# Dynamic convolution into a gated MLP on one core: tiles taken from 8 on, group 0 one step ahead of group 1, all seven taps added by TensorE

## Chip, core and metric

The kernel runs on one NeuronCore of a Trainium2 chip. The metric is the device time of one execution, in microseconds; lower is better. The time before the change is 1306.71 us, the median of 3 runs (1306.46 to 1307.04).

## What is computed

The input `x` is 4 batches of 4096 positions of 192 numbers. For each position and each of 8 heads, seven weights are made by a softmax, and the 24 numbers of the head are the weighted sum of the last seven positions. The result goes, as 16384 tokens of 192 numbers, through a gated MLP with 1536 hidden units. The weights of the MLP arrive as float64.

```python
w = exp(weight_gen - max(weight_gen, axis=-1))          # [4, 4096, 8, 7]
w = w / (sum(w, axis=-1) + 1e-9)
x_pad = concatenate([zeros(B, 6, D), x], axis=1)
att[b, s, h, :] = sum over k of w[b, s, h, k] * x_pad[b, s + k, h, :]
g, v = att @ w_gate, att @ w_val                        # 192 -> 1536
out = (g * sigmoid(g) * v) @ w_out                      # 1536 -> 192
```

## The kernel before

**Tiles.** Partition p holds the 128 consecutive tokens 128p to 128p+127; tile t is token t of every partition, so there are 128 tiles of 128 tokens, and a tap's earlier position is the tile before, in the same partition. Tiles 0 to 5 need the last six tiles of the partition before (the halo, PAD = 6); at the start of a batch the halo is zero. Four tiles (JG) make a group; there are 32 groups. `x` is loaded in chunks of 8 tiles (`load_x`), the softmax weights in chunks `wcuts` of 12 and then 24 tiles (`load_taps`).

**Steps.** The hidden units are cut into 12 blocks (NF) of 128. One step (g, f) takes block f of group g: `up_first` and `up_second` make 18 matmuls in row pairs into two PSUM banks (of four, so two steps are in flight), ScalarE does `silu` (L522), VectorE multiplies (`gated`, L531 for groups 0 and 1, L536 after them), and two steps later (LAG) `down` (L570 for groups 0 and 1, L581 and L590 after them) adds the block into the output. The list `steps` gives the order: with HEAD = 4, group 0 takes four steps alone, then groups 1 and 0 take turns, and from step 24 on groups 2 to 31 follow one by one.

**What lies beside the steps.** `todo[i]` is a list of small operations that are issued with step i: the first through `between` ahead of the step's product on VectorE, the others after it. Every engine works in the order of issue. The lists hold: the conversion of a weight block from float64 (`weight_ops`: five parts, six instructions on VectorE and three on ScalarE, L415 to L474, and the load of the block four further on); `split` of the output weights (L405, L406); the attention of the next group on VectorE (`attention_ops`: seven products at L230 and six additions at L251) with its transposition through DRAM (`turn_ops`); the softmax of the next chunk (`softmax_ops`); and loads. The exponentials of a chunk stand together in one step (`exps`), since they need another table on ScalarE than silu.

**Groups 0 and 1** are transposed by TensorE instead (`summed_turn`): VectorE makes a tap's product into a tile `xatt` (three buffers), ScalarE copies 64 of its columns to the end (`twice`, L304), and `turn` (L309) multiplies its four tiles by the identity in 8 matmuls (16 records in the trace) that add into two PSUM banks. `SUMS` says which taps VectorE adds first: group 0 has five turns for seven taps (two additions, L300), group 1 has four (three additions). `split_ops` then makes the high part (ScalarE, L370) and the low part (VectorE, L377) of the sum.

**The prologue** is everything issued before step 0: the loads, the softmax of the first chunk, the taps of group 0 with weight block 0 between them, and block 1 and part of 2. In before, group 1's taps lie in steps 0 to 3. The first chunk of `x` needs its halo at once: four memsets on GpSimd (L149) and eight DMAs (L152).

Of the kernel before, what the change touches and what calls it, by code (L numbers as in the profile page):

```python
# [18 lines left out]
def dynconv_glu_kernel(  # L19
# [41 lines left out]
    EXP1 = 16  # L61
    LOAD1 = 1
# [3 lines left out]
    HEAD = 4  # L66
    SUMS = {0: ((0,), (1,), (2,), (3, 4), (5, 6)), 1: ((0, 1), (2, 3), (4, 5), (6,))}
# [39 lines left out]

    xcuts = cut([2 * JG])
    wcuts = cut([3 * JG, 6 * JG])
# [10 lines left out]
    def load_taps(c):  # L120

        j0, n = wcuts[c]
        wt = w_t[c] = soft.tile([P, NJ, H, K], F32, tag="wt", name="wt")
        pieces = {0: (0, JG, n), 1: range(0, n + 1, 2 * JG)}.get(c, (0, n))

        def load(a, b):
            nc.sync.dma_start(
                out=wt[:, a:b].rearrange("p t h k -> p t (h k)"), in_=wgr[:, j0 + a : j0 + b]
            )

        return [lambda a=a, b=b: load(a, b) for a, b in zip(pieces, pieces[1:])]

    def load_x(c):

        j0, n = xcuts[c]
        xt = x_t[c] = xin.tile([P, PAD + NX, D], F32, tag="xt", name="xt")
        pieces = {0: (0, JG, n), 1: range(0, n + 1, 2)}.get(c, (0, n))

        def load(a, b):
            own = PAD if c and a == 0 else 0  # L140
            nc.sync.dma_start(
                out=xt[:, PAD + a - own : PAD + b], in_=xr[:, j0 + a - own : j0 + b]
            )
            if c == 0 and a == 0:
# [3 lines left out]
                for p0 in range(0, P, per):  # L148
                    nc.gpsimd.memset(xt[p0 : p0 + 1, 0:PAD], 0.0)  # L149
# [8 lines left out]
    def softmax_ops(c):  # L158
# [3 lines left out]
        def cuts(m):  # L162
            return [slice(j, min(j + m, n)) for j in range(0, n, m)]
# [44 lines left out]
        if c == 0:  # L208
            before = [
                op  # L210
                for p in (slice(0, JG), slice(JG, n))
                for op in each(p, (largest, less, exponentials))
            ]
        else:
            before = [op for p in cuts(PIECE) for op in each(p, (largest, less))]
        after = [op for p in cuts(PIECE if c else JG) for op in each(p, (total, inverse, normal))]
# [57 lines left out]
    def summed_turn(g):  # L274
# [6 lines left out]

        parts = SUMS[g]

        def tap(n):
            a = {}

            def product(k, first):
                def go():
                    if first:
                        a["sum"] = att.tile([P, JG, 2 * P], F32, tag="xatt", name="xatt", bufs=3)  # L290
                        mul(nc.vector, k, a["sum"][:, :, 0:D])
                    else:
                        a["other"] = att.tile([P, JG, D], F32, tag="prod", name="prod")
                        mul(nc.vector, k, a["other"])

                return go

            def add():
                x = a["sum"][:, :, 0:D]
                nc.vector.tensor_tensor(out=x, in0=x, in1=a.pop("other"), op=ALU.add)  # L300

            def twice():
                x = a["sum"]
# [252 lines left out]
    def down(g, f, pair, second):  # L556
# [49 lines left out]
        if lo is None:  # L606
            if pair:
# [5 lines left out]
                nc.sync.dma_start(out=outr[:, g * JG : (g + 1) * JG], in_=osb[:, :, 0:D])  # L613
# [14 lines left out]
        for t in range(JG):  # L628
            nc.sync.dma_start(
                out=blocks[:, t0:t1, g * JG + t], in_=osb[t * Q : (t + 1) * Q, t0:t1, 0:D]  # L630
# [12 lines left out]
    with tc.manual_schedule():  # L643
        nc.gpsimd.memset(exp_bias, -920.0 * TWO23)

        load_weights(0, nc.scalar)
        nc.scalar.activation(out=warm, in_=exp_bias, func=AF.Exp)
        now, soon = load_x(0)
        for op in load_taps(0) + [now]:
            op()  # L650
        load_weights(1)
        soon()
# [5 lines left out]
        for op in before:  # L658
            op()
        convert = [weight_ops(f) for f in range(NF)]  # L660
        w0, w1, w2, w3 = convert[:4]
        nc.scalar.activation(out=warm, in_=exp_bias, func=AF.Silu)
        for op in after[:6]:
            op()
        ps, taps = summed_turn(0)

        def tap(n):
            made, turn = taps[n]
            return made + [turn]

        turns = split_ops(0, ps)
# [122 lines left out]
```

## Time and profile before

| | us |
|---|---|
| median of 3 runs | 1306.71 |
| the profiled execution | 1305.82 |
| its span, first to last instruction | 1304.0 |
| TensorE busy | 1271.4 |
| VectorE busy | 1015.6 |
| ScalarE busy | 577.6 |

The profile is of one execution. PE is TensorE's matmuls, PEld its weight loads, DVE is VectorE, ACT ScalarE, POOL GpSimd, SP the queue that issues most DMAs. A matmul's end is modelled, and two matmuls of a row pair run beside each other, so a busy TensorE is not by itself a TensorE at its peak; the distance from one step's first matmul to the next step's is the sounder measure. The granted clock of TensorE has two levels, 1.00 (2.4 GHz) and 0.50 (1.2 GHz).

### The profile page before, as it was taken

To read this page: it belongs to the slowest core of one execution; us is meant where nothing else is said; L and a number is where in the kernel's file an instruction comes from. 1 tells how busy PE (TensorE), PEld (TensorE's weight loads), DVE (VectorE), ACT (ScalarE), POOL (GpSimd) and SP (SyncE) were. 2 spreads that over 40 slices of the span, in tenths; PEclk is the share of its full clock that TensorE was granted. 3 is DMA by queue.
4 is the path that set the end of the run, shared out by engine and by line. 5 is a ranking of instruction groups with operands and counts; after the bars stand their busy time and mean duration, and the time that the engine had idled before them with its cause. 6 is when DMAs were issued, how large, how long until landed. Compare 5 with 4: busy or idle time off the path is not lost.

```text
span 1304.0 us, 31222 instructions
## 1 busy us (share of the span) xinstructions
PE 1271.4 (97%) x13200; PEld 1226.0 (94%) x13200; DVE 1015.6 (78%) x1438; ACT 577.6 (44%) x1010; POOL 4.9 (0%) x11
## 2 busy tenths in 40 slices
PE   4998999999999999999999999999999999999997
PEld 3787988999999999999999999999999999999997
DVE  7798688777788877788877778877778877777843
ACT  3344344544444445444444544444454444444443
POOL 1000000000000000000000000000000000000000
PEclk9899999999999999999999999999999999999999
DMA  5332211212212121211212121121211212111010
GB/s 161 115 102 63 84 29 27 84 29 84 63 33 65 42 71 42 84 47 31 82 30 83 42 73 37 48 78 36 84 42 26 71 42 72 42 42 42 17 38 13
DMA packets 64149, 74.88 MB, mean 57 GB/s; under 512 B 6924, under 2 KB 53516, under 8 KB 62216
## 3 DMA queue, kind: packets, MB, share of 16 engines
q1 hardware_dynamic: 63416, 72.30, 20.1%
q8 instruction: 103, 1.69, 0.5%
q10 hardware_dynamic: 592, 0.59, 0.2%
q14 instruction: 38, 0.31, 0.1%
HBM read 48.48 MB, written 24.38 MB: 56 GB/s over the span
## 4 chain that ended last, share of the span: by engine, by line
PE 86%; DVE 8%; ACT 3%; DMA 2%; issue 1%; SPq 0%; ACTq 0%; DVEq 0%
PE up L502 22%; PE up L514 22%; PE dn L581 20%; PE up L505 18%; PE dn L590 3%; DVE prod L230 1%; DVE h L536 1%; PE dn L570 1%; DVE xatt L230 1%; DVE hi L531 1%; ACT sg L522 1%; DVE e L450 1%; DVE m L439 1%; DVE w L461 1%; ACT L522 0%
## 5 line engine op out<-in xcount | busy, mean ns | idle before, releaser
L581 PE MATMUL dn<-wo,hi 64*128 64x384 f32 x2880 | 550.6, 344 | 0.4 <-ACT hi L537 0.4
L590 PE MATMUL dn<-wo,lo 64*128 64x192 f32 x2880 | 485.4, 249 | 0.3 <-DVE lo L539 0.3
L581 PEld LDWEIGHTS dn<-wo,hi 64*128 64x128 f32 x2880 | 445.8, 184 | 8.8 <-ACT osb L619 1.4
L590 PEld LDWEIGHTS dn<-wo,lo 64*128 64x128 f32 x2880 | 427.4, 186 | 3.2 <-DVE lo L539 0.5
L536 DVE TENSOR_TENSOR h<-up,sg 128x512 f32<-128x512 f32 x360 | 247.6, 688 | 179.3 <-ACT sg L522 179.1
L537 ACT ACTIVATE hi<-h 128x512 fp32r<-128x512 f32 x360 | 227.7, 633 | 358.7 <-DVE h L536 358.6
L522 ACT ACTIVATE sg<-up 128x512 f32<-128x512 f32 x384 | 228.3, 594 | 305.5 <-PE up L514 296.8
L539 DVE TENSOR_TENSOR lo<-h,hi 128x512 fp32r<-128x512 f32 x360 | 246.3, 684 | 80.2 <-ACT hi L537 80.2
L502 PE MATMUL up<-xhi,w_hi 64*128 64x512 f32 x768 | 214.9, 420 | 7.1 <-ACT sg L522 2.5
L514 PE MATMUL up<-xhi,w_hi 64*128 64x512 f32 x768 | 213.3, 421 | 0.2
L505 PE MATMUL up<-xhi,w_hi 64*128 64x512 f32 x768 | 202.0, 391 | 2.0 <-ACT xhi L370 2.0
L502 PE MATMUL up<-xhi,w_lo 64*128 64x512 f32 x768 | 203.7, 395 | 0.0
L502 PE MATMUL up<-xlo,w_hi 64*128 64x512 f32 x768 | 202.6, 391 | 0.3 <-DVE xlo L377 0.2
L505 PE MATMUL up<-xhi,w_lo 64*128 64x512 f32 x768 | 201.9, 391 | 0.0
L514 PE MATMUL up<-xhi,w_lo 64*128 64x512 f32 x768 | 201.3, 390 | 0.0
L505 PE MATMUL up<-xlo,w_hi 64*128 64x512 f32 x768 | 201.1, 388 | 0.2 <-DVE xlo L377 0.2
L514 PE MATMUL up<-xlo,w_hi 64*128 64x512 f32 x768 | 200.5, 387 | 0.0
L230 DVE TENSOR_TENSOR prod<-xt,wt 128x768 f32<-128x768 f32 x185 | 175.7, 950 | 0.2
L251 DVE TENSOR_TENSOR xatt<-xatt,prod 128x768 f32<-128x768 f32 x180 | 170.7, 948 | 0.0
L502 PEld LDWEIGHTS up<-xhi,w_hi 64*128 64x128 f32 x768 | 120.7, 184 | 11.3 <-ACT w_hi L470 3.5
L505 PEld LDWEIGHTS up<-xhi,w_hi 64*128 64x128 f32 x768 | 120.7, 185 | 6.8 <-ACT xhi L370 2.5
L505 PEld LDWEIGHTS up<-xlo,w_hi 64*128 64x128 f32 x768 | 120.9, 185 | 4.7 <-DVE xlo L377 0.5
(54 smaller groups left out, 1246.9 us busy)
## 6 DMA issues: line engine op xcount, KB each, us to landing
xt<-in_x_dram SPq DMA_DIRECT2D x14, 1344.0 KB, 7.2
turned<-cut SPq DMA_DIRECT2D x120, 96.0 KB, 2.0
out_dram<-osb SPq DMA_DIRECT2D x116, 96.0 KB, 1.9
t<-turned SPq DMA_DIRECT2D x60, 128.0 KB, 2.7
t<-turned SPq DMA_DIRECT2D x30, 256.0 KB, 3.0
raw<-in_moe_w_out_dram SPq DMA_DIRECT2D x11, 192.0 KB, 2.7
wt<-in_weight_gen_dram SPq DMA_DIRECT2D x3, 672.0 KB, 4.6
raw<-in_moe_w_gate_dram SPq DMA_DIRECT2D x11, 128.0 KB, 2.2
```

What stands on the lines that cost most here:

```text
L230: engine.tensor_tensor(out=into.rearrange("p t (h i) -> p t h i", h=H), in0=src, in1=w, op=ALU.mult)
L251: nc.vector.tensor_tensor(out=a, in0=a, in1=tmp.pop(k), op=ALU.add)
L439: nc.vector.scalar_tensor_tensor(out=st["m"], in0=st["raw"][:, :, 0], scalar=28, in1=st["m"], op0=ALU.logical_shift_right, op1=ALU.bitwise_or,
L502: nc.tensor.matmul(ps, w[r, fs], m[r], start=(n == 0), stop=False)
L505: ins = nc.tensor.matmul(sums[i], w[r, i, fs], m[r], start=False, stop=False)
L514: ins = nc.tensor.matmul(sums[i], w[r, i, fs], m[r], start=False, stop=(n == len(full) - 1))
L522: nc.scalar.activation(out=sg, in_=sums[0], func=AF.Silu)
L536: nc.vector.tensor_tensor(out=h, in0=sums[1], in1=sg, op=ALU.mult)
L537: nc.scalar.activation(out=hi, in_=h, func=AF.Copy)
L539: nc.vector.tensor_tensor(out=lo, in0=h, in1=hi.bitcast(F32), op=ALU.subtract)
L581: nc.tensor.matmul(acc[g, t], hi[r, cs], wo[r, f].rearrange("p a d -> p (a d)"), start=opens, stop=False,)
L590: nc.tensor.matmul(acc[g, t][:, 0:D], lo[r, cs], wo[r, f, 0], start=False, stop=closes)
```

## The change

- **Order of the tiles.** `place` adds 8 tiles (TURN), modulo 128. Group 0 takes tiles 8 to 11, and its halo is tiles 2 to 7 of the same partition, loaded with them. Tiles 0 to 7, with the halo from the partition before, are the last chunk; its zeros are a memset on VectorE.
- **Order of the steps.** HEAD is 1: (0,0), (1,0), (0,1), (1,1) and so on. A weight block then serves two steps in a row from the start. In step 0 the first six operations of its list go ahead of the product (FIRST).
- **Taps of groups 0 and 1.** No additions on VectorE: seven products, seven copies and seven turns for each group. Group 1's first three products are issued ahead of step 0, everything else of its taps, its `split_ops` and weight block 1 in step 0.
- **Softmax.** The first chunk has 24 tiles, the next two 28, the last two 24. All exponentials of the first chunk are in the prologue, in slices of 4, 4, 8 and 8 tiles, and the silu table is loaded after them. The normalisation of the last two slices lies in steps 1 to 7. The next chunk's softmax lies in steps 31 to 56, its load at step 12.
- **Output weights.** `split` of block f moves to step 23 + f.
- **Start.** ScalarE's first table load comes ahead of its five weight DMAs; SP's order is two pieces of softmax weights, two of `x`, weight block 1, the rest of `x` and of the softmax weights, blocks 2 and 3.

```diff
-    EXP1 = 16
-    LOAD1 = 1
+    TURN = 2 * JG
-    HEAD = 4
-    SUMS = {0: ((0,), (1,), (2,), (3, 4), (5, 6)), 1: ((0, 1), (2, 3), (4, 5), (6,))}
+    HEAD = 1
+    FIRST = 6
+    def place(at):
+        return (at + TURN) % T
-    wcuts = cut([3 * JG, 6 * JG])
+    wcuts = cut([6 * JG, 7 * JG, 7 * JG, 6 * JG])
...
-        pieces = {0: (0, JG, n), 1: range(0, n + 1, 2)}.get(c, (0, n))
+        pieces = {0: (0, JG + 1, PAD + JG, PAD + n), 1: range(0, PAD + n + 1, 2)}.get(c, (0, PAD + n))
+        if at == 0:
+            pieces = (PAD, PAD + n)
...
-            if c == 0 and a == 0:
+            if at == 0:
-                for p0 in range(0, P, per):
-                    nc.gpsimd.memset(xt[p0 : p0 + 1, 0:PAD], 0.0)
+                nc.vector.memset(xt[:, 0:PAD], 0.0)
...
-            made = [product(k, m == 0) for m, k in enumerate(parts[n])]
-            return made + [add] * (len(made) - 1) + [twice], turn
+            return [product, turn]
-        return ps, [tap(n) for n in range(len(parts))]
+        return ps, [tap(n) for n in range(K)]
...
-            while between() and g == 0 and f < HEAD:
-                pass
+            for _ in range(FIRST if g == 0 and f < HEAD else 1):
+                between()
...
+        nc.scalar.activation(out=warm, in_=exp_bias, func=AF.Exp)
         load_weights(0, nc.scalar)
-        nc.scalar.activation(out=warm, in_=exp_bias, func=AF.Exp)
-        now, soon = load_x(0)
-        for op in load_taps(0) + [now]:
+        taps_in, x_in = load_taps(0), load_x(0)
+        for op in (*taps_in[0:2], *x_in[0:2]):
             op()
         load_weights(1)
-        soon()
+        for op in (x_in[2], taps_in[2]):
+            op()
...
+        for op in before[0:6] + after[0:3]:
             op()
         for op in (
-            tap(0) + w0[0:1] + tap(1) + w0[1:2] + tap(2) + w0[2:4] + tap(3) + w0[4:5]
-            + tap(4) + w1[0:3] + turns[0:2] + w1[3:4] + turns[2:4] + w1[4:5] + w2[0:2]
+            taps[0] + w0[0:1] + taps[1] + after[3:6] + taps[2] + w0[1:2] + taps[3] + taps[4] + w0[2:3]
+            + taps[5] + taps[6] + w0[3:4] + before[6:7] + split_ops(0, ps) + w0[4:5] + before[7:]
         ):
             op()
+        nc.scalar.activation(out=warm, in_=exp_bias, func=AF.Silu)
...
+        for tap in taps1[:3]:
+            tap[0]()
+        todo[0] = [tap[1] for tap in taps1[:3]] + [op for tap in taps1[3:6] for op in tap]
+        todo[0] += w1[0:1] + taps1[6]
+        todo[0] += w1[1:3] + split_ops(1, ps1) + w1[3:5]
...
+        spread(load_x(1), 0, 4)
+        todo.setdefault(1, []).extend(after[6:9])
+        spread(after[9:], 3, 9)
         for f in range(NF):
-            todo.setdefault(max(due[f] + 3, HEAD + 6), []).append(
+            todo.setdefault(2 * NF - 1 + f, []).append(
                 lambda f=f: split(wo[:, f, 0], wo[:, f, 1], wo32[:, f])
             )
+        todo.setdefault(NF, []).extend(load_taps(1))
         for c in range(1, len(wcuts)):
-            s0 = (wcuts[c - 1][0] // JG - 1) * NF - LEAD if c > 1 else NF
+            s0 = max((wcuts[c - 1][0] // JG - 1) * NF - LEAD, 2 * NF + 4)
...
-            if i in turns:
-                turns[i]()
```

## Rows read from the trace of the kernel before

**Rows 1.** The page, part 1: busy time, share of the span and instructions.
```profile
PE 1271.4 (97%) x13200; PEld 1226.0 (94%) x13200; DVE 1015.6 (78%) x1438; ACT 577.6 (44%) x1010; POOL 4.9 (0%) x11
```

**Rows 2.** Engines by stretch: length, busy time and instructions, granted clock, DMA.
```profile
30.00:40.00 10.00, 8.29 (x36) 6.34 (x38) 9.68 (x14) 3.03 (x7) 0.00 (x0) 0.54 0.22 62
...
100.00:110.00 10.00, 6.32 (x55) 4.81 (x54) 6.58 (x13) 6.78 (x9) 0.00 (x0) 1.00 0.00 2
...
160.00:180.00 20.00, 20.00 (x212) 17.92 (x211) 19.01 (x27) 9.76 (x19) 0.00 (x0) 1.00 0.12 47
...
260.00:280.00 20.00, 19.77 (x206) 18.80 (x204) 12.53 (x18) 10.20 (x16) 0.00 (x0) 1.00 0.23 52
```

**Rows 3.** Timeline: start, length, instruction; first matmuls of steps 0, 4, 12, 18, 20, 24.
```profile
24.66 0.50 PE L502 MATMUL up<-xhi,w_hi 64*128 64x512 f32 x2
...
54.52 0.51 PE L502 MATMUL up<-xhi,w_hi 64*128 64x512 f32 x2 [1.11 <-ACT xhi L370]
...
81.98 0.53 PE L502 MATMUL up<-xhi,w_hi 64*128 64x512 f32 x2
...
108.42 0.50 PE L502 MATMUL up<-xhi,w_hi 64*128 64x512 f32 x1 [2.53 <-ACT sg L522]
...
116.45 0.54 PE L502 MATMUL up<-xhi,w_hi 64*128 64x512 f32 x2
...
129.93 0.53 PE L502 MATMUL up<-xhi,w_hi 64*128 64x512 f32 x2
```

**Rows 4.** Timeline of the prologue, up to the split of group 0's sum.
```profile
3.59 4.96 SPq L152 DMA_DIRECT2D xt<-in_x_dram  x8
...
7.21 0.39 DVE L200 TENSOR_TENSOR wt<-wt,sm 128x224 f32<-128x224 f32 x1
...
10.60 0.96 DVE L230 TENSOR_TENSOR xatt<-xt,wt 128x768 f32<-128x768 f32 x1 [1.48 <-DMA raw<-in_moe_w_gate_dram]
...
12.12 6.91 PEld L309 LDWEIGHTS tr<-ident,xatt 128*128 128x128 f32 x48 [12.12 <-issue]
...
22.67 2.05 PE L309 MATMUL tr<-ident,xatt 128*128 128x128 f32 x16 [1.15 <-ACT xatt L304]
...
23.87 0.60 ACT L370 ACTIVATE xhi<-tr 128x512 fp32r<-128x512 f32 x1 [0.58 <-PE tr L309]
```

**Rows 5.** Weight loads of turns: mean (13 to 14 us), two timelines, clock by stretch.
```profile
L309 PEld LDWEIGHTS tr<-ident,xatt 128*128 128x128 f32 x7 | 1.6, 333 | 0.0
...
33.15 3.49 PEld L309 LDWEIGHTS tr<-ident,xatt 128*128 128x128 f32 x16 [2.32 <-ACT xatt L304]
...
45.82 1.86 PEld L309 LDWEIGHTS tr<-ident,xatt 128*128 128x128 f32 x16 [0.22 <-issue]
...
39.00:39.25 0.25, 0.25 (x4) 0.07 (x2) 0.25 (x1) 0.00 (x0) 0.00 (x0) 0.72 0.00 0
```

**Rows 6.** Groups by shape, 0 to 115 us: busy us, mean ns, idle before.
```profile
L531 DVE TENSOR_TENSOR hi<-up,sg 128x512 f32<-128x512 f32 x19 | 13.0, 685 | 6.5 <-ACT sg L522 6.3
...
L230 DVE TENSOR_TENSOR xatt<-xt,wt 128x768 f32<-128x768 f32 x10 | 9.5, 952 | 1.5 <-DMA raw<-in_moe_w_gate_dram 1.5
...
L439 DVE SCALAR_TENSOR_TENSOR m<-raw,m 128x576 int32<-128x576 int32 x12 | 9.0, 750 | 0.1
...
L474 DVE TENSOR_TENSOR w_lo<-w,w_hi 128x384 fp32r<-128x384 f32 x12 | 6.7, 555 | 2.4 <-ACT w_hi L470 2.4
L415 DVE TENSOR_SCALAR e<-raw 128x576 int32<-128x576 int32 x12 | 5.4, 453 | 0.0
...
L377 DVE TENSOR_TENSOR xlo<-tr,xhi 128x512 fp32r<-128x512 f32 x4 | 2.7, 688 | 3.5 <-ACT xhi L370 3.5
...
L177 DVE TENSOR_TENSOR wt<-wt,mx 128x448 f32<-128x448 f32 x1 | 0.6, 624 | 0.0
```

**Rows 7.** ScalarE's timeline around the exponentials of step 16: the two table loads.
```profile
103.84 1.28 ACT L183 ACT_TABLE_LOAD   x1
...
106.48 1.28 ACT L522 ACT_TABLE_LOAD   x1
```

More of the change, by code (lines that the diff above doesn't have):

```diff
@@ L123, in load_taps @@
         wt = w_t[c] = soft.tile([P, NJ, H, K], F32, tag="wt", name="wt")
-        pieces = {0: (0, JG, n), 1: range(0, n + 1, 2 * JG)}.get(c, (0, n))
+        pieces = {0: (0, JG, 2 * JG, n), 1: (0, n // 2, n)}.get(c, (0, n))
+        wrap = T - TURN - j0
+        if 0 < wrap < n:
+            pieces = (0, wrap, n)
         def load(a, b):
+            at = place(j0 + a)
             nc.sync.dma_start(
-                out=wt[:, a:b].rearrange("p t h k -> p t (h k)"), in_=wgr[:, j0 + a : j0 + b]
+                out=wt[:, a:b].rearrange("p t h k -> p t (h k)"), in_=wgr[:, at : at + b - a]
             )
@@ L160, in softmax_ops, with cuts @@
         n = wcuts[c][1]
-        def cuts(m):
-            return [slice(j, min(j + m, n)) for j in range(0, n, m)]
+        def cuts(m, first=0):
+            edges = [j for j in (0, first) if j < m] if first else [0]
+            edges = sorted({*edges, *range(0, n, m), n})
+            return [slice(j, k) for j, k in zip(edges, edges[1:])]
         st = {}
@@ L210, in softmax_ops @@
                 op
-                for p in (slice(0, JG), slice(JG, n))
+                for p in cuts(2 * JG, JG)
                 for op in each(p, (largest, less, exponentials))
@@ L215, in softmax_ops @@
             before = [op for p in cuts(PIECE) for op in each(p, (largest, less))]
-        after = [op for p in cuts(PIECE if c else JG) for op in each(p, (total, inverse, normal))]
+        after = [op for p in (cuts(PIECE) if c else cuts(2 * JG, JG)) for op in each(p, (total, inverse, normal))]
         return before, exponentials, after
@@ L280, in summed_turn, with product @@
             ps = [ps_dn.tile([P, NC], F32, tag=f"dn{2 + n}", name=f"tr{n}") for n in range(2)]
-        parts = SUMS[g]
         def tap(n):
             a = {}
[L287 to L303, printed above, removed]
+            def product():
+                a["tap"] = att.tile([P, JG, 2 * P], F32, tag="xatt", name="tap", bufs=3)
+                x = a["tap"]
+                mul(nc.vector, n, x[:, :, 0:D])
                 nc.scalar.activation(out=x[:, :, D:], in_=x[:, :, P:D], func=AF.Copy)
             def turn():
+                x = a["tap"]
                 for half in (1, 0):
@@ L629, in down @@
             nc.sync.dma_start(
-                out=blocks[:, t0:t1, g * JG + t], in_=osb[t * Q : (t + 1) * Q, t0:t1, 0:D]
+                out=blocks[:, t0:t1, place(g * JG) + t], in_=osb[t * Q : (t + 1) * Q, t0:t1, 0:D]
             )
@@ L657, in dynconv_glu_kernel @@
         before, exponentials, after = softmax_ops(0)
-        for op in before:
-            op()
[L660 to L671, printed above, removed]
+        convert = [weight_ops(f) for f in range(NF)]
+        w0, w1 = convert[:2]
+        ps, taps = summed_turn(0)
+        for op in before[0:6] + after[0:3]:
+            op()
         for op in (
-            tap(0) + w0[0:1] + tap(1) + w0[1:2] + tap(2) + w0[2:4] + tap(3) + w0[4:5]
-            + tap(4) + w1[0:3] + turns[0:2] + w1[3:4] + turns[2:4] + w1[4:5] + w2[0:2]
+            taps[0] + w0[0:1] + taps[1] + after[3:6] + taps[2] + w0[1:2] + taps[3] + taps[4] + w0[2:3]
+            + taps[5] + taps[6] + w0[3:4] + before[6:7] + split_ops(0, ps) + w0[4:5] + before[7:]
         ):
             op()
+        nc.scalar.activation(out=warm, in_=exp_bias, func=AF.Silu)
         steps = [(0, f) for f in range(HEAD)]
```

30 lines of the change are left out of this document (10 added, 20 removed).

## The prediction

> **What bounds the kernel now.** I read the page's busy shares first, then the engines by stretch, then TensorE's timeline for the start of each step, and last the timelines of the other engines in the first 110 us. TensorE is busy 97% of the span [rows 1], so a gain can only come from stretches in which it isn't at its pace. By stretches, everything from step 24 on is full: 160 to 180 us shows 20.00 of 20 us while VectorE does 19.01 beside it [rows 2]. What is left is the start. The step starts [rows 3] tell it: steps 20 to 24 go from 116.45 to 129.93, 3.37 us a step, and that is TensorE's own pace in groups 0 and 1. Steps 4 to 12 take 27.46 us, 3.43 a step, near that pace. But steps 0 to 4 take 29.86 us, and steps 12 to 18 take 26.44 us where six steps at 3.37 are 20.2. The first loss is VectorE's taps, sums and weight blocks (9.68 busy of 10 us between 30 and 40, TensorE at clock 0.54 [rows 2]); the second is the same engine with softmax and output weights on top, and at its end the exponentials of step 16, which held TensorE 2.53 us [rows 3, 7]. Ahead of step 0 lie 24.66 us, and 10.60 of these end with the first product waiting for a DMA (the releaser's name is of another transfer; the eight halo DMAs were issued from 3.59 to 8.55 [rows 4]). Step 24 at **129.93** is therefore the mark: the steps behind it are the same work in both kernels, so the gain is how much earlier step 24 starts. I work that out from the start of the span.
>
> **First product.** The halo DMAs go from the front of SP's queue; two pieces of softmax weights and two of `x` are issued instead, four issues of about 0.6 us each by the eight in 4.96 [rows 4]. The softmax of four tiles ended at 7.60 in before (7.21 + 0.39 [rows 4]); VectorE now has 4 tiles ahead of it instead of 8, which saves less than two times 0.62 [rows 6], and ScalarE still issues its five weight DMAs first, behind the table load. I take 6.9. Bounds: 6.9, and the 10.60 of before if `x` lands no sooner.
>
> **Group 0's turns.** From product to first turn 10.60 to 12.12, 1.52 us [rows 4]: the first turn at 8.4. All seven turns now follow each other on TensorE. In before, 48 loads took 6.91 us [rows 4], with loads of 333 ns at first, the slow clock's length [rows 5], up to about 15.2. So 3.1 us ran at half clock, which loses 1.55, and the rest gives (6.91 - 0.19 - 1.55) / 48 = 0.108 us a load, 1.75 us for a turn of 16 in a row (a turn by itself spans 1.86 [rows 5]). VectorE's product is 0.95 [rows 6], so TensorE sets the pace, although weight block 0 stands between the taps: 7 products, 3.7 us of block 0 and 1.4 of softmax end before the last turn. The last turn starts at 8.4 + 1.55 + 6 * 1.75 = 20.5. The two additions saved for group 0 (0.95 each) give nothing more. From a last turn to step 0's first matmul: 22.67 to 24.66, 1.99 us [rows 3, 4]. Step 0 starts at 22.5 instead of 24.66.
>
> **Step 0 and the silu table.** The last exponentials, then the table, then group 1's copies stand in one queue on ScalarE. The high part starts 1.2 us after the last turn's start, at 21.7, and takes 0.60 [rows 4]. VectorE then does two low parts (0.69), the low part of weight block 0 (0.555) and three softmax operations on 8 tiles (0.62 each) [rows 6]: 3.8 us less 0.08 of overlap for each, 3.4, so 25.7. Then an exponential (0.6, the size of the high part), a table load of 1.28 [rows 7], the warming call 0.2 and the first copy 0.42 with its hand-over: group 1's first turn at 28.4. TensorE has only step 0's nine pairs between 22.3 and 28.4.
>
> The exponentials and the switch behind them are priced from the trace: the second load began 106.48 - 103.84 - 1.28 = 1.36 us after the first ended, and that is the exponential itself [rows 7]. The Trainium skill (ScalarE: Activation LUTs, What ACT_TABLE_LOAD costs) adds a drain of some 1.38 us to each 1.283 us load; the load's length agrees and the drain isn't in these rows. By that rule group 1's first turn would come 1.4 us later and the forecast would be 1300.8 instead of 1299.4.
>
> **Group 1's turns: seven instead of four, in one row.** Each product waits for the turn three before it (three buffers); behind it on VectorE are the product of step 0 and weight block 1, both needed only in step 2. At full clock the last turn starts at 28.4 + 6 * 1.75 = 38.9 and step 1 at 40.9. The clock decides what comes on top. In before it fell at about 28.9 after thin work and was back at 39.1 [rows 5], TensorE working without a break from 33.15: 5.95 us at half clock, 3.0 us lost; a turn then took 3.49 instead of 1.86 [rows 5]. The thin stretch of the new kernel, 22.3 to 28.4, is about as empty as the one before that fall, so I expect the clock to fall again. Bounds of the loss: 0 (no fall), 1.55 (as at the first turns), 3.0; I take 2.3. Step 1 at **43.2**.
>
> **Steps 1 to 24.** Step 1 makes nine pairs. Step 2 needs weight block 1, whose last instructions stand behind the low parts of group 1: high part 0.60 (starting 0.8 before step 1), two low parts, two of 0.75, the copy of the high weights about 0.5 [rows 4, 6]: 3.9 us after step 1. From there VectorE and TensorE are nearly level. For two steps VectorE has one weight block (2 * 0.45 + 3 * 0.75 + 0.555 = 3.71), two products of 0.685, and 13/15 of a tap operation a step at 0.95: 6.73, less 0.08 for each of ten, 5.95 us [rows 6], against TensorE's 6.74. In steps 1 to 7 two slices of normalisation come on top, 1.4 us for 4 tiles (the normalisation that ended at 7.60 [rows 4]), so 1.4 to 2.8 for 8; with 2.0 each, VectorE needs 6.95 a pair there. I put steps 2 to 4 at 7.5 (silu of step 1 stands behind a weight block's ScalarE part), 4 to 10 at 3 * 6.95 = 20.85, and 10 to 24 at 14 * 3.37 = 47.2. Step 24: 43.2 + 3.9 + 7.5 + 20.85 + 47.2 = **122.65**, 7.3 us ahead of 129.93.
>
> **What I cost at nothing.** The output weights move to steps 23 to 34 (0.35 each on VectorE) and the next chunk's 28 tiles to steps 31 to 56; their cover is a TensorE that stayed full beside 19.01 of 20 us on VectorE [rows 2]. Without that cover it is up to 4 us (rival). Exponentials within full groups cost 0.23 us of TensorE time [rows 2], and there are four after step 24 in either kernel. The halo moves to the last chunk of `x`: a memset on VectorE of some 1 us and eight DMAs, 4.96 us of SP [rows 4]; behind them in SP's queue are an output transfer and, nine steps (29 us) later, the transposition of group 28. If that cover failed it would cost those 5 us once.
>
> **Sum.** The profiled execution is 1305.82, span 1304.0; 7.3 less is 1298.5. The median lies 0.9 above that execution, so 1306.71 - 7.3 = **1299.4**.
>
> **Rivals.**
> - *The clock doesn't fall* before group 1's turns: 2.3 us more, gain 9.6, 1297.1. For: in before a gap of 2.53 us at 106 to 108 left it at 1.00 [rows 2, 3]. Against: the work before that gap was dense, here it isn't. Chance 0.22.
> - *The start doesn't move*: the first product still waits for `x`, up to 3.7 us later, since the bytes ahead of it are about as many as before. Gain 3.6, 1303.1. This is the change not doing what it says. Against: half of the wait was issue time of eight DMAs. Chance 0.18.
> - *The moved work comes back*: VectorE falls behind in steps 24 to 56 with output weights and 28 tiles in 28 steps; 4 us, 1303.4. Against: rows 2. Chance 0.10.
> - *Slower: the clock stays at half through all of group 1's turns.* Seven turns at 3.49 instead of 1.86 cost 11.4 us against the 9.6 of gain without a fall: 1.8 slower, 1308.5. It decides from about 19 us of dense work at half clock on. Against: in before 5.95 us were enough to bring it back. Chance 0.06.
>
> **Chances.** The forecast has 0.44. The range goes from 1295.0 (no fall, VectorE not late in steps 4 to 10 and step 0's table wait shorter: 2 us better than the first rival) to 1304.5 (the second and third rival with 1 us of their own spread). About 0.2% (2.6 us) is what a measurement can tell. Faster by more than that: 0.44 + 0.22 and two thirds of the 0.28 of the middle rivals, 0.85; within it 0.09; slower 0.06.
>
> **What the profile after would show.** The first product at about 7 and the first turn at 8.4; step 0 at 22.5; group 1's first turn at 28.4 right after a table load; a clock of 0.50 for some 4 to 5 us then; step 1 at 43; step 10 near 75; step 24 near 122.7; no table load between there and step 43; TensorE without idle time after step 24. I'd be wrong if step 24 starts later than 127, or if the distance from step 24 to the end is not the 1174.1 us of before (1304.0 - 129.93).

## The result and the profile after

The changed kernel is slower: 1322.01 us (median of 4 runs, 1320.76 to 1323.29) against 1306.59 for the kernel before in the same comparison, a ratio of 1.0119 (95% interval 1.0101 to 1.0136). The forecast was 1299.4.

The page, part 1 (busy time, share of the span, instructions):

```profile
span 1319.7 us, 31389 instructions
...
PE 1287.7 (98%) x13280; PEld 1246.8 (94%) x13280; DVE 1013.9 (77%) x1442; ACT 575.3 (44%) x1014; POOL 0.7 (0%) x7
```

Against [rows 1], TensorE's share has gone up a point in a kernel that is 1.2% slower. The five turns added (80 more records) and matmuls at half clock count as busy like any other, so the share tells nothing here; the starts of the steps do. The timeline of the start, and the first matmuls of steps 0, 1, 10, 23, 24 and 39 (start, length, instruction, idle time before it and what ended that):

```profile
8.09 0.96 DVE L240 TENSOR_TENSOR tap<-xt,wt 128x768 f32<-128x768 f32 x1 [1.98 <-DMA xt<-in_x_dram]
...
9.61 13.93 PEld L305 LDWEIGHTS tr<-ident,tap 128*128 128x128 f32 x112 [9.61 <-issue]
...
23.66 0.50 PE L497 MATMUL up<-xhi,w_hi 64*128 64x512 f32 x2
...
29.87 14.03 PEld L305 LDWEIGHTS tr<-ident,tap 128*128 128x128 f32 x112 [2.43 <-ACT tap L299]
...
44.03 0.50 PE L497 MATMUL up<-xhi,w_hi 64*128 64x512 f32 x2
...
76.48 0.54 PE L497 MATMUL up<-xhi,w_hi 64*128 64x512 f32 x2
...
120.37 0.53 PE L497 MATMUL up<-xhi,w_hi 64*128 64x512 f32 x1
...
124.90 0.52 PE L497 MATMUL up<-xhi,w_hi 64*128 64x512 f32 x1
...
179.22 0.41 PE L497 MATMUL up<-xhi,w_hi 64*128 64x512 f32 x1
```

The start did gain. Step 23 comes at 120.37 where before has it at 126.56, 6.18 us earlier; the forecast had some 7.3. Step 24 is 5.03 earlier (129.93 [rows 3]), and step 39 is already later than before's 178.62. The engines by stretch (length, busy time and instructions of PE, PEld, DVE, ACT and POOL, granted clock, DMA share, GB/s) show where the rest went:

```profile
160.00:180.00 20.00, 17.61 (x168) 15.10 (x166) 18.06 (x27) 8.14 (x17) 0.00 (x0) 1.00 0.09 38
...
400.00:420.00 20.00, 17.93 (x166) 16.05 (x162) 15.15 (x22) 11.79 (x19) 0.00 (x0) 0.91 0.00 1
...
680.00:700.00 20.00, 18.13 (x166) 16.52 (x164) 15.34 (x22) 12.06 (x19) 0.00 (x0) 0.91 0.00 1
```

The stretch from 160 to 180, full in before [rows 2], has lost 2.4 us, and two stretches far behind the edited part, both 20.00 at 1.00 in before, lose 2 us each and a tenth of the clock besides.

I add the losses up from the steps' starts: the length of a stretch of steps, less 3.37 us for each step up to 26 and 3.21 us for each behind it (TensorE's own pace in the two kinds of group; 3.2117 in the column from step 56 on, since 12 steps take 38.54). From the last step's start to the end it is 14.4 to 14.7 us, but 15.1 in softmax_early and 15.4 in split_late. The table is of the profiled executions; the last two columns are span and median (or the one time there is).

| kernel | step 0 starts | step 23 starts | over pace, 23 to 39 | 39 to 56 | 56 to 383 | span | time |
|---|---|---|---|---|---|---|---|
| before | 24.66 | 126.56 | 0.22 | 0.0 | 6.22 | 1304.0 | 1306.6 |
| after | 23.66 | 120.37 | 7.01 | 3.87 | 17.30 | 1319.7 | 1322.0 |
| exp_block3 | 25.18 | 122.06 | 6.99 | 3.91 | 7.50 | 1311.6 | 1312.9 |
| before_block10 | 24.85 | 127.31 | 0.70 | 0.54 | 14.83 | 1314.4 | 1316.2 |
| exp_sweep | 25.36 | 122.26 | 8.57 | 3.11 | 12.28 | 1317.4 | 1319.2 |
| wo_early | 25.12 | 124.17 | 2.22 | 3.93 | 15.73 | 1317.2 | 1318.9 |
| wo_last | 24.32 | 121.22 | 2.94 | 3.88 | 16.96 | 1316.1 | 1319.4 |
| softmax_early | 24.63 | 121.51 | 6.53 | 3.90 | 16.68 | 1320.3 | 1322.1 |
| two_adds | 23.03 | 117.75 | 7.02 | 3.88 | 14.97 | 1314.7 | 1316.5 |
| split_late | 25.46 | 122.36 | 7.21 | 3.87 | 16.38 | 1321.9 | 1323.7 |
| five_mended | 23.16 | 118.22 | 2.24 | 2.43 | 7.80 | 1302.0 | 1303.8 |
| six_mended | 23.18 | 118.73 | 1.05 | 3.15 | 10.0 | 1304.2 | 1305.5 |
| best | 22.90 | 119.42 | 0.66 | 2.41 | 7.90 | 1301.7 | 1303.4 |

After against before: 6.18 gained up to step 23; then 6.8, 3.9 and 11.1 us lost, and 0.1 at the end: 15.7, the difference of the spans. Of the 11.1, single steps carry 9.8: 4.7 in steps 105 to 112 and 5.1 in steps 180 to 196, around the exponentials of steps 106 and 190. The other 1.3 are a net of losses under 0.9 us each.

The 6.18 are in part this execution's luck. exp_block3, exp_sweep, wo_last, softmax_early and split_late have the same start as after, yet their step 0 comes at 24.32 to 25.46 and their step 23 at 121.22 to 122.36, 4.2 to 5.3 us ahead of before. The weight loads of group 0's turns between 14 and 15 us, in after and then in split_late, show where after is ahead:

```profile
L305 PEld LDWEIGHTS tr<-ident,tap 128*128 128x128 f32 x11 | 1.3, 192 | 0.0
```

```profile
L305 PEld LDWEIGHTS tr<-ident,tap 128*128 128x128 f32 x6 | 1.4, 333 | 0.0
```

At 333 ns they still have the slow clock's length [rows 5]; between 17 and 18 us the mean is 192 ns in both.

### The profile page after: what moved, and what is told of

The parts are those of the page before. It is cut to its first block, busy times and chain, and to the rows that moved or that the text cites. A ratio compares the mean times of both kernels' runs of the same rounds, so it can differ in the third digit from the quotient of the medians.

```text
span 1319.7 us, 31389 instructions
## 1 busy us (share of the span) xinstructions
PE 1287.7 (98%) x13280; PEld 1246.8 (94%) x13280; DVE 1013.9 (77%) x1442; ACT 575.3 (44%) x1014; POOL 0.7 (0%) x7
## 4 chain that ended last, share of the span: by engine, by line
PE 78%; DVE 13%; ACT 5%; issue 1%; DMA 1%; SPq 0%; ACTq 0%; DVEq 0%
PE up L497 20%; PE up L509 20%; PE dn L576 17%; PE up L500 16%; DVE h L531 3%; DVE prod L240 2%; PE dn L585 2%; PE dn L565 2%; DVE xatt L261 2%; DVE lo L534 2%; ACT hi L532 2%; PE tr L305 1%; DVE xlo L372 1%; ACT sg L517 1%; DVE xatt L240 1%
## 5 line engine op out<-in xcount | busy, mean ns | idle before, releaser
L576 PE MATMUL dn<-wo,hi 64*128 64x384 f32 x2880 | 573.4, 345 | 2.6 <-ACT osb L614 1.9
L585 PE MATMUL dn<-wo,lo 64*128 64x192 f32 x2880 | 507.9, 249 | 0.3 <-DVE lo L534 0.3
L576 PEld LDWEIGHTS dn<-wo,hi 64*128 64x128 f32 x2880 | 476.5, 185 | 11.8 <-ACT osb L614 5.6
L585 PEld LDWEIGHTS dn<-wo,lo 64*128 64x128 f32 x2880 | 451.2, 187 | 1.3 <-DVE lo L534 0.5
L497 PE MATMUL up<-xhi,w_hi 64*128 64x512 f32 x768 | 228.3, 422 | 9.1 <-ACT sg L517 3.7
L509 PE MATMUL up<-xhi,w_hi 64*128 64x512 f32 x768 | 222.6, 421 | 0.2
L497 PE MATMUL up<-xhi,w_lo 64*128 64x512 f32 x768 | 213.9, 395 | 0.9 <-DVE w_lo L469 0.9
L497 PE MATMUL up<-xlo,w_hi 64*128 64x512 f32 x768 | 214.3, 393 | 0.2
L500 PE MATMUL up<-xhi,w_hi 64*128 64x512 f32 x768 | 212.0, 390 | 0.0
L500 PE MATMUL up<-xhi,w_lo 64*128 64x512 f32 x768 | 211.9, 390 | 0.0
L500 PE MATMUL up<-xlo,w_hi 64*128 64x512 f32 x768 | 211.0, 388 | 0.0
L509 PE MATMUL up<-xhi,w_lo 64*128 64x512 f32 x768 | 210.5, 390 | 0.0
L509 PE MATMUL up<-xlo,w_hi 64*128 64x512 f32 x768 | 209.7, 388 | 0.0
L497 PEld LDWEIGHTS up<-xhi,w_hi 64*128 64x128 f32 x768 | 130.0, 184 | 17.0 <-DVE h L531 8.4
L497 PEld LDWEIGHTS up<-xhi,w_lo 64*128 64x128 f32 x768 | 130.2, 184 | 5.3 <-DVE w_lo L469 2.5
L500 PEld LDWEIGHTS up<-xlo,w_hi 64*128 64x128 f32 x768 | 130.4, 185 | 3.7 <-DVE xlo L372 0.4
(54 smaller groups left out, 1317.4 us busy)
```

The lines of the kernel that those rows point to most:

```text
L497: nc.tensor.matmul(ps, w[r, fs], m[r], start=(n == 0), stop=False)
L500: ins = nc.tensor.matmul(sums[i], w[r, i, fs], m[r], start=False, stop=False)
L509: ins = nc.tensor.matmul(sums[i], w[r, i, fs], m[r], start=False, stop=(n == len(full) - 1))
L576: nc.tensor.matmul(acc[g, t], hi[r, cs], wo[r, f].rearrange("p a d -> p (a d)"), start=opens, stop=False,)
L585: nc.tensor.matmul(acc[g, t][:, 0:D], lo[r, cs], wo[r, f, 0], start=False, stop=closes)
```

## The experiments

The expectations use these names. **PLACE**: the exponentials of a chunk cost little or much by the block of the group in which they stand; chunks of 28 tiles move them from block 3 (steps 63, 135, 207 and 279 in before) to blocks 7, 10, 10 and 3 (steps 43, 106, 190, 267). **SIZE**: its rival, 28 tiles instead of 24 make them dear. **COPY WAIT**: the output weights, split in full groups, hold VectorE until ScalarE has copied them. **SOFTMAX**: its rival, the 28 tiles crowd VectorE there. **TURNS**: TensorE's 14 turns cost more than the additions saved. **BUFFER**: at step 23 the split of group 2 waits for a buffer that group 0 still reads.

### The exponentials: place or size

ScalarE's timeline in after, step 106, which starts at 399.32, with its silu (`sg`), and behind it VectorE's product and the first two matmuls of step 108, which take the two banks of step 106:

```profile
401.94 0.63 ACT L532 ACTIVATE hi<-h 128x512 fp32r<-128x512 f32 x1 [1.88 <-DVE h L531]
402.48 0.62 ACT L365 ACTIVATE xhi<-t 128x512 fp32r<-128x512 f32 x1
403.12 1.28 ACT L193 ACT_TABLE_LOAD   x1
404.41 1.52 ACT L193 ACTIVATE wt<-wt 128x1568 f32<-128x1568 f32 x1
405.94 1.28 ACT L517 ACT_TABLE_LOAD   x1
407.24 0.60 ACT L517 ACTIVATE sg<-up 128x512 f32<-128x512 f32 x1
407.87 0.69 DVE L531 TENSOR_TENSOR h<-up,sg 128x512 f32<-128x512 f32 x1 [3.10 <-ACT sg L517]
407.89 0.49 PE L497 MATMUL up<-xhi,w_hi 64*128 64x512 f32 x1 [1.83 <-ACT sg L517]
...
408.61 0.79 PE L497 MATMUL up<-xhi,w_hi 64*128 64x512 f32 x1 [0.23 <-DVE h L531]
```

Two loads and the exponentials of 28 tiles are 4.1 us wherever they stand. Here they begin 3.80 us after the step's start, since two copies stand ahead of them on ScalarE, and the first of these waits for VectorE. The silu comes 7.9 us after the step's start, and TensorE, whose four banks hold two steps, that is 6.42 us of work, runs dry: one bank is free when the silu ends, the other when the product behind it does, at 408.56. exp_block3 moves the exponentials back to block 3 and leaves the 28 tiles.

```diff
             at = s0 + (s1 - s0) * 5 // 8 - 2
+            at -= (at - 3) % NF if c > 1 else 0
```

> The exponentials of the third and fourth chunk move from steps 106 and 190 (hidden block 10 of their group) to 99 and 183 (block 3, where the kernel before has all of its own); 28 tiles as in the changed kernel. Theory PLACE: at block 10 ScalarE and VectorE have the split of the next group's sum and two products of the attention after it in front, so the exponentials start a step late, silu waits, TensorE stands still and its clock falls. Then the stretches of steps 106 to 111 and 190 to 195, which now lose 4.7 and 4.4 us against 3.21 a step, lose at most 0.7 each, the clock stays at 1.00 there, and the time goes from 1322.0 to about 1313.5. Rival SIZE: 28 tiles instead of 24 (1.52 us instead of 1.32) are what is too long; then the loss moves to steps 99 and 183, and the time stays within 1320 to 1322.

Measured: 1312.89 us (1312.0 to 1313.78), 1.0047 of before (1.0031 to 1.0064), 9.1 us less than after. ScalarE at step 99, which starts at 378.47:

```profile
379.75 0.63 ACT L532 ACTIVATE hi<-h 128x512 fp32r<-128x512 f32 x1 [0.85 <-DVE h L531]
380.41 1.28 ACT L193 ACT_TABLE_LOAD   x1
381.70 1.52 ACT L193 ACTIVATE wt<-wt 128x1568 f32<-128x1568 f32 x1
383.24 1.28 ACT L517 ACT_TABLE_LOAD   x1
384.53 0.60 ACT L517 ACTIVATE sg<-up 128x512 f32<-128x512 f32 x1
```

The same 1568 elements and the same two loads, but the load starts 1.94 us after the step's start and the silu at 6.06; steps 98 to 101 lose 0.88 us instead of the 4.21 of steps 105 to 108 in after. The converse, block 10 with the 24 tiles of before, in the kernel before:

```diff
+            at += 7 if c in (2, 3) else 0
             if c + 1 < len(wcuts):
```

> The kernel before with one thing changed: the exponentials of chunks 2 and 3 (24 tiles each) stand seven steps later, at steps 70 and 142 (block 10 instead of 3). Theory PLACE: 3 to 5 us lost at each, 2.0 of it only where the clock falls, against 0.6 at block 3: time 1312 to 1315. Rival SIZE: 24 tiles fit wherever they stand, time within 1 us of 1306.4.

Measured: 1316.19 us, 9.6 slower than before; 8.6 of the 10.4 us by which its span is longer lie behind step 56. ScalarE at step 70, and the engines just after the exponentials of steps 70 and 142:

```profile
284.26 1.28 ACT L183 ACT_TABLE_LOAD   x1
285.56 1.33 ACT L183 ACTIVATE wt<-wt 128x1344 f32<-128x1344 f32 x1
...
288.20 0.60 ACT L522 ACTIVATE sg<-up 128x512 f32<-128x512 f32 x1
```

```profile
288.00:292.00 4.00, 2.92 (x20) 2.39 (x22) 3.17 (x5) 1.91 (x4) 0.00 (x0) 0.86 0.00 0
...
526.00:530.00 4.00, 2.41 (x20) 1.90 (x22) 2.67 (x4) 2.41 (x4) 0.00 (x0) 1.00 0.00 0
```

Steps 69 to 72 lose 4.07 and steps 141 to 144 lose 2.56 at the same block with the same work: the first time the clock falls after TensorE's stand-still, the second time it doesn't. The 24 tiles' exponentials take 1.33 instead of 1.52, so size is worth 0.2. PLACE holds, SIZE is refuted. A sweep puts the four exponentials at blocks 3, 0, 6 and 9 and gives the law:

```diff
+            at += {1: -4, 2: -10, 3: -4, 4: 6}[c]
```

> Of the changed kernel only the steps of the exponentials are moved: chunk 2 from 43 to 39 (block 3), chunk 3 from 106 to 96 (block 0), chunk 4 from 190 to 186 (block 6), chunk 5 from 267 (block 3) to 273 (block 9). Theory PLACE: the loss grows with the work in front of the exponentials in that step, which is least at blocks 2 to 4 and most at 9 and 10 (attention and split): under 0.7 at step 39, about 1 at 96 (the output copies of the group before stand there), about 0.5 to 1 at 186, 3 to 5 at 273 although that chunk has 24 tiles. Rival SIZE: 273 loses no more than the 0.6 that 267 lost, and 96 and 186 lose 2 or more each.

It missed three of the four numbers: step 39 lost 1.67 where under 0.7 was expected, step 96 lost 3.68 instead of about 1, and step 273 lost 1.42 instead of 3 to 5. So it is not the block as such that sets the price. The delay from the step's start to its silu, and the loss of four steps, counted from the step before, in the kernels named:

| block | silu after | loss | seen at steps |
|---|---|---|---|
| 3 | 5.65 to 6.06 | 0.47 to 0.88 | 63, 135, 207, 279 (before); 267 (after); 99, 183 (exp_block3) |
| 6 | 6.04 | 0.84 | 186 (exp_sweep) |
| 7 | 6.30 | 1.14 | 43 (after) |
| 9 | 6.61 | 1.42 | 273 (exp_sweep) |
| 0 | 7.38 | 3.68 | 96 (exp_sweep) |
| 10 | 7.69 to 7.91 | 2.56, or 4.0 to 4.2 with a clock fall | 106, 190 (after); 70, 142 (before_block10) |

The loss is a straight line, the delay less 5.2 us (0.47 at 5.65, 0.84 at 6.04, 1.42 at 6.61, 2.56 at 7.74): two steps in flight are 6.42 us, and the product behind the silu ends 1.3 us after the silu starts (407.24 to 408.56 above). Two things come on top. At block 10 it is the fall of the clock, some 1.5 us. At step 96 it is 1.5 us in step 98, with the clock at 1.00, where TensorE waits for the output copies of the group before:

```profile
383.08 0.82 PE L576 MATMUL dn<-wo,hi 64*128 64x384 f32 x2 [0.57 <-ACT osb L614]
```

The sweep's step 39 lost 3.63 at 6.86, but 1.96 of that in step 38, ahead of the exponentials; steps 39 to 41 lost 1.67, on the line.

### What fills steps 23 to 39

After's timeline in step 36, VectorE's and ScalarE's rows and one of TensorE's:

```profile
166.69 0.68 DVE L531 TENSOR_TENSOR h<-up,sg 128x512 f32<-128x512 f32 x1
167.41 0.63 ACT L532 ACTIVATE hi<-h 128x512 fp32r<-128x512 f32 x1 [2.86 <-DVE h L531]
167.43 0.49 PE L497 MATMUL up<-xhi,w_hi 64*128 64x512 f32 x1 [0.96 <-DVE h L531]
167.95 0.35 ACT L400 ACTIVATE wo<-wo 128x192 fp32r<-128x192 f32 x1
168.33 0.36 DVE L401 TENSOR_TENSOR wo<-wo,wo 128x192 fp32r<-128x192 f32 x1 [0.95 <-ACT wo L400]
168.60 0.69 DVE L534 TENSOR_TENSOR lo<-h,hi 128x512 fp32r<-128x512 f32 x1
```

The first operation of a step's list goes between VectorE's product `h` and its low part `lo`. When that operation is the split, its copy stands on ScalarE behind the high part of `h`, and VectorE, in order, sits idle for 0.95 us. The view of waits counts it (us, times, the longest):

```profile
DVE wo L401 <- ACT wo L400: 11.0, 12, 1.0
```

In before this wait came once, 0.9 us: there the splits lie in groups 0 and 1, whose steps make no high part. Three runs tell it from the softmax. One splits the output weights twelve steps earlier:

```diff
-            todo.setdefault(2 * NF - 1 + f, []).append(
+            todo.setdefault(NF - 1 + f, []).append(
```

> Of the changed kernel only the split of the output weights is moved: block f from step 23 + f to step 11 + f, so that all lie in the steps of groups 0 and 1. Theory COPY WAIT: in a step of a full group the split stands between the product and its low part, and VectorE waits 0.95 us for ScalarE's copy, which stands behind the high part; with the softmax of 28 tiles this makes VectorE late in steps 31 to 38. Then the 4.5 us lost in steps 35 to 38 shrink below 1.5 and the 2.2 us lost at steps 23 and 26 by about 1: time 1318. Rival SOFTMAX: the softmax alone is too much there, at least 3.5 of the 4.5 us stay: 1321. A loss of up to 1 us in steps 11 to 22 is possible in both, since VectorE does 13.8 of 20 us there.

Measured: steps 23 to 39 lose 2.22 instead of 7.01, but steps 4 to 23 lose 3.31 instead of 1.15; 1318.94 us. One loads the 28 tiles at step 8 and spreads their softmax from step 15 on, with its exponentials still at 43:

```diff
-        todo.setdefault(NF, []).extend(load_taps(1))
+        todo.setdefault(8, []).extend(load_taps(1))
-            s0 = max((wcuts[c - 1][0] // JG - 1) * NF - LEAD, 2 * NF + 4)
+            s0 = max((wcuts[c - 1][0] // JG - 1) * NF - LEAD, NF)
...
```

> Of the changed kernel only the second chunk's softmax ahead of its exponentials is spread over steps 15 to 42 instead of 31 to 42 (its load at step 8 instead of 12); the exponentials stay at step 43, the output weights at steps 23 to 34. Theory SOFTMAX: six instructions of 0.85 us packed into 12 steps are what makes VectorE late at 35 to 38; the 4.5 us go below 1, time 1317.5. Rival COPY WAIT: the output weights' waits suffice, at least 2.5 us stay in steps 23 to 38. In both the 2.8 us of steps 48 to 50 (normalisation) stay.

Measured: 6.53 us lost in steps 23 to 39, 1322.12 us, the wait unchanged at 11.0 us: SOFTMAX is refuted. (Steps 35 to 38 lose 2.53 instead of 4.53, but steps 26 and 32 lose 1.56 more: the loss moves with the softmax as long as the waits are there.) The last one changes neither work nor step, only where the split stands in each step's list: the loop that adds it comes behind the loop over the groups, so an operation of the next group's attention goes ahead of it.

> Of the changed kernel only the place of the output weights' split within a step is changed: same steps 23 to 34, same instructions, but last in the step's list and so behind the low part of the product instead of ahead of it. Theory COPY WAIT: VectorE no longer waits 0.95 us in each of these steps for ScalarE's copy; the 7.0 us lost in steps 23 to 39 fall below 3.5, time 1318 to 1319. Rival LOAD: it is the work (12 instructions of 0.36 us and six softmax instructions) that is too much, and at least 5.5 us stay.

Measured: 2.94 us instead of 7.01, and the wait once instead of twelve times:

```profile
167.57 0.35 DVE L401 TENSOR_TENSOR wo<-wo,wo 128x192 fp32r<-128x192 f32 x1
...
168.44 0.84 DVE L180 TENSOR_REDUCE mx<-wt 128x96 f32<-128x672 f32 x1
169.22 0.69 DVE L534 TENSOR_TENSOR lo<-h,hi 128x512 fp32r<-128x512 f32 x1
```

```profile
DVE wo L401 <- ACT wo L400: 0.9, 1, 0.9
```

While ScalarE makes the high part, VectorE now has something else to do, and the wait is gone in all steps but one. COPY WAIT holds: 4.1 us of the 6.8, by order alone. What is left is 1.16 us at step 23 (below), 0.52 at step 26 and 1.16 at step 38; the last two stay open. (wo_last's time is 3.3 above its span, so it is read by steps.)

### Step 23 and the buffer

After's rows for the split of group 2, which step 24 needs:

```profile
118.03 0.63 ACT L365 ACTIVATE xhi<-t 128x512 fp32r<-128x512 f32 x1 [3.05 <-PE up L497]
118.69 0.69 DVE L372 TENSOR_TENSOR xlo<-t,xhi 128x512 fp32r<-128x512 f32 x1 [3.19 <-ACT xhi L365]
...
121.78 0.50 PE L497 MATMUL up<-xhi,w_hi 64*128 64x512 f32 x1 [0.88 <-DVE hi L526]
```

Both engines stand still for 3 us until TensorE lets go of the buffer. With groups 0 and 1 taking turns to the end, group 0's last step is 22; in before it is 19. First I only made the split two steps later for group 2:

```diff
-            spread(halves, at + 3, at + 5)
+            late = 2 if g == 2 else 0
+            spread(halves, at + 3 + late, at + 5 + late)
```

> Of the changed kernel only the split of group 2's sum is moved, from steps 20 and 21 to 22 and 23. Theory BUFFER: its high part takes the buffer that group 0's sum had, which the last step of group 0 (now step 22, in before step 19) still reads; ScalarE waits for that with silu behind it, and VectorE for ScalarE; the 1.16 us lost at step 23 go below 0.4. Rival: they stay, since VectorE's first products of group 3 are what is late. Time 1321 or unchanged at 1322.

Measured: nothing gained, 1323.66 us. Step 23's loss of 1.16 is gone, and step 24 loses 1.60, as TensorE now waits for the split itself:

```profile
127.18 0.50 PE L500 MATMUL up<-xhi,w_hi 64*128 64x512 f32 x2 [0.47 <-ACT xhi L365]
...
128.26 0.50 PE L500 MATMUL up<-xlo,w_hi 64*128 64x512 f32 x2 [0.58 <-DVE xlo L372]
```

So this run alone does not decide. A third buffer (below, in six_mended and best) lets the split stand early: steps 23 to 39 then lose 1.05 and 0.66. BUFFER holds.

### The turns

```diff
+    SUMS = ((0,), (1,), (2,), (3, 4), (5, 6))
...
```

Taps 3 and 4, and 5 and 6, are added by VectorE again: five turns for each group.

> Of the changed kernel only the taps are changed back in part: groups 0 and 1 have five turns on TensorE instead of seven, and VectorE adds taps 3 and 4, and 5 and 6 (two additions a group). Theory TURNS: TensorE sets the pace of the taps (seven turns in a row took 14.0 us in either group), so two turns fewer let step 0 start up to 2 us earlier (23.7 to about 22) and step 1 about 4 us earlier (44.0 to about 40); step 24 at 120.5 to 121.5 instead of 124.9; time about 1318. Rival ADDS: VectorE's four additions of 0.95 us come back on the path; step 24 at 125 to 127, time 1322 to 1324.

Measured: step 1 at 41.23 instead of 44.03, 2.8 earlier, and 1316.53 us. From step 0 to step 1 it is 18.20 instead of 20.37, so 2.2 us are the two turns saved in group 1, and 0.6 an earlier step 0. (The five kernels named above with seven turns take 20.5 us from step 0 to step 1 and start step 0 at 24.32 to 25.46, the four with five turns at 22.90 to 23.18; so group 0's two turns are worth between 0.5 us, against after itself, and 2.6.) Of the 5.5 us by which the time is lower than after's, 2.3 lie behind step 56, where nothing was changed. The turns of group 0, then group 1's in two rows:

```profile
9.92 6.86 PEld L314 LDWEIGHTS tr<-ident,tap 128*128 128x128 f32 x48 [9.92 <-issue]
...
29.09 8.85 PEld L314 LDWEIGHTS tr<-ident,tap 128*128 128x128 f32 x64 [2.41 <-ACT tap L308]
...
39.24 1.86 PEld L314 LDWEIGHTS tr<-ident,tap 128*128 128x128 f32 x16 [1.31 <-ACT tap L308]
```

An addition at 0.95 us [rows 6] takes the place of a turn at 1.86 (the last row) or more. TURNS holds for group 1, at about half the size that I expected.

### The parts together

five_mended takes two_adds, softmax_early, exponentials in block 3 throughout, the split late for group 2, and the output weights by twos, from step 11 on:

```diff
-            todo.setdefault(2 * NF - 1 + f, []).append(
+            todo.setdefault(NF - 1 + f // 2 * 2, []).append(
...
+            at -= (at - 3) % NF
```

> The changed kernel with five things put otherwise: exponentials of every later chunk at block 3 (steps 39, 99, 183, 267); the second chunk's load at step 8 and its softmax from step 15 on; the output weights two by two in the odd steps 11 to 21, where no weight block's conversion stands ahead of the copy on ScalarE; two additions on VectorE per group; the split of group 2's sum in steps 22 and 23 instead of 20 and 21. Theory (each loss has its own place and they add): step 24 at 119.5 to 120.5, steps 23 to 39 lose 1.5 instead of 7.0, steps 39 to 56 lose 1.2 instead of 3.9, step 56 to the end 7.5 instead of 17.3: time 1301, faster than the kernel before (1306.4) by 4 to 6 us. Rival (what leaves one place turns up at another, since VectorE has no room in steps 11 to 56): 1306 to 1311.

Measured: 1303.76 us, 0.9979 of before (0.9970 to 0.9988), 18.2 less than after and 2.8 above the forecast: step 24 came at 121.59, and the three stretches lost 2.24, 2.43 and 7.80, each more than expected, so the losses do not quite add. Next the third buffer, and the later softmax in slices of 8 tiles instead of 12:

```diff
-    PIECE = 3 * JG
+    PIECE = 2 * JG
...
+        hi = [xts.tile([P, NC], F32R, tag=f"xhi{half}", name="xhi", bufs=3) for half in range(2)]
```

> Like five_mended, but the split of group 2's sum stands in steps 20 and 21 again and has a third buffer for its high and low parts; to make room, the later softmax goes in slices of 8 tiles instead of 12. Theory BUFFER: moving the split by two steps only traded one wait (for group 0's last reader) for another (step 24 waiting for the low part), and with a third buffer neither is left: the 1.57 us at step 24 go below 0.3 and none come at step 23; the smaller slices take some of the 2.4 us between steps 39 and 56. Time 1301.5 to 1302.5 against 1303.8. Rival: VectorE's order itself is late at steps 20 to 24, and 1 us or more stays there: 1303 to 1304.

Measured: 1305.46 us, 0.9990 (0.9981 to 0.9999). The buffer does its work (1.05 instead of 2.24), but steps 39 to 56 lose 0.7 us more and those behind 2.2, where only the slices differ; it is slower than either expectation. best goes back to 12 tiles, keeps the third buffer for the high parts, and takes the first of these normalisations off the steps around 50:

```diff
+            if c == 1:
+                for n, op in enumerate(after):
+                    todo.setdefault(41 + n + (4 if n > 6 else 0) - (n > 10), []).append(op)
...
+                halves = [halves[n] for n in (0, 2, 1, 3)]
+                todo.setdefault(at + 4, []).extend(halves[:2])
+                todo.setdefault(at + 5, []).extend(halves[2:])
```

> Like five_mended, with softmax slices of 12 tiles, and two things more: a third buffer for the high parts alone (group 2's high parts in step 21, its low parts in step 22, when group 0's last step has been read), and the second chunk's normalisation kept out of steps 48 to 51, where the output copies of the group before stand. Theory BUFFER with the place of the normalisation: the 1.57 us at step 24 go below 0.5 and the 1.19 us at step 50 below 0.4; time 1301.5 to 1302.5. Rival: the waits only change their step, as when the split was moved: 1303.5 or more.

Measured: 1303.40 us (1301.72 to 1303.91, 7 runs), 0.9973 of before (0.9962 to 0.9985), which is not clear of five_mended's 0.9979. Its stretches beside [rows 2] and after's:

```profile
30.00:40.00 10.00, 8.36 (x63) 8.05 (x63) 7.32 (x10) 1.58 (x4) 0.00 (x0) 0.90 0.00 0
...
160.00:180.00 20.00, 19.73 (x201) 18.89 (x199) 16.50 (x24) 12.12 (x19) 0.00 (x0) 1.00 0.10 22
400.00:420.00 20.00, 20.00 (x215) 19.38 (x214) 17.96 (x25) 9.54 (x17) 0.00 (x0) 1.00 0.10 21
```

The holes at 160 and 400 us are closed (the exponentials behind the second now stand at 368 us and lose 0.88), the 1.57 us of step 24 are gone, and the clock between 30 and 40 is 0.90 instead of the 0.54 of before. Step 50 still loses 1.14 us (1.19 in five_mended, 1.94 in after), although the normalisation no longer stands there: that reason is refuted, and what makes step 50 late stays open.

## Why the prediction was wrong

- **The step that failed** is "the steps behind it are the same work in both kernels, so the gain is how much earlier step 24 starts". From step 24 to the end it is 1194.8 us (1319.7 - 124.90) where I carried over 1174.1: 20.7 of the 24.7 us between the forecast of the profiled execution, 1298.5, and the 1323.2 it took (the rest is step 24, 2.25 us later than forecast, and a time that lies 3.5 us above its span instead of 1.8). Only TensorE's work is the same behind step 24: the output weights and 12 tiles' softmax have come over from ahead of it, and the exponentials stand at other places. By stretch the 20.7 are 5.6 up to step 39, 3.9 up to step 56 and 11.1 behind it.
- **"Exponentials within full groups cost 0.23 us"** was the idle time in one stretch around block 3 [rows 2]. Step by step they cost 0.47 to 0.88 there, and I never asked at which block the new chunks would put them: they stand five eighths of the way between two chunks, less 2 steps, which is 43 of 72 steps for 24 tiles and 50 of 84 for 28: seven blocks further on. In block 10 they cost 4.0 to 4.2, twice. No rival covered it. exp_block3 and before_block10 show it from both sides.
- **"What I cost at nothing."** The cover, VectorE at 19.01 of 20 us beside a full TensorE, hides work that waits for no other engine. The split waits for a copy that ScalarE has only behind the high part, and that order exists in full groups alone. The rival "the moved work comes back" had the place and the sign; its 4 us were 6.8 up to step 39 and 3.9 behind it, and its 0.10 was too little. Of the 3.9, 1.14 are the exponentials at step 43 and 2.65 steps 49 and 50.
- **A buffer was not in the sum.** Turns taken to step 23 keep group 0's high part in use until step 22: step 23's 1.16 us.
- **The start** was right in kind and some 1.1 us late in this execution, more in the others like it (step 0 at 24.32 to 25.46, with the slow loads shown above). The first product came at 8.09 instead of 6.9, waiting 1.98 us for `x`; step 0 at 23.66 instead of 22.5; group 1's first turn at 29.87 instead of 28.4. The clock did fall: 0.50 from 29.5 to 32.9, of which 3.1 us behind the first turn, a loss of 1.5 where I took 2.3. Step 1 came at 44.03 (43.2), step 10 at 76.48 (some 75.5). (The terms that I listed from step 1 to step 2 add up to 3.2 us and not to 3.9; it was 3.50.) The gain without the moved parts would have been some 4 to 6 us, less than the 9.6 of the best case and more than the second rival's 3.6.
- **That the additions saved would give nothing** was right, and more than right: as turns they cost 2.2 us in group 1.
- **The table switch** was priced rightly. A load of 1.28 us is followed by the next activation 0.01 to 0.02 us later (403.12, 404.41; 405.94, 407.24). The Trainium skill (ScalarE: Activation LUTs, What ACT_TABLE_LOAD costs) would put a drain of 1.38 us behind each; these rows have none.

## What to carry to other kernels

When a size is changed from which places follow (a chunk, a group, a lead), write down at which place each dear step will land, and work out from that place when its result is needed: exponentials with two table loads, 4.1 us in all, cost under 1 us or over 4 here, by how late the next silu came: what it came later than 5.2 us after its step's start was lost, and more where the clock fell. A busy share is a cover only for work that waits for no other engine; for a step with a hand-over, look at what stands ahead of the partner's half in the partner's queue. A gain at the start is safe only when the steps behind it keep their places, so compare the starts of the steps over the whole span, and first of all where nothing was meant to change.

## What the runs showed of the hardware

The clock after a stand-still was not the same from one execution to the next. Around step 190 the same exponentials at the same block in after and in two_adds give these stretches:

```profile
688.00:692.00 4.00, 4.00 (x30) 3.78 (x28) 3.29 (x5) 0.97 (x3) 0.00 (x0) 0.57 0.01 4
```

```profile
682.00:686.00 4.00, 3.26 (x29) 2.73 (x31) 3.51 (x5) 1.57 (x3) 0.00 (x0) 1.00 0.00 0
```

In after the clock fell and step 192 lost 2.05 us; in two_adds it stayed, and the step lost 0.60. So a fall costs some 1.45 us on top of the stand-still in that step, and a stall can cost half as much again in a profile as it did in the one beside it; 0.4 us of it comes back, since the six steps from 190 on lose 4.50 and 3.45. Of the six kernels with these exponentials at steps 106 and 190, the clock fell behind step 106 in all, behind step 190 in all but two_adds and wo_early. What decides between them stays open.
